# The w2 sums of the last ten tiles in 3.5 pairs of passes in place of four, with an order searched anew

## The chip, the cores and the metric

The kernel runs on one core of a Trainium2 chip. The metric is the device time of one execution in microseconds; the median of three runs of the kernel before is 189.86 us (189.66 to 190.07). Its work is bf16 with sums in f32, for one sequence of 2048 tokens and width 448.

## The reference, cut to what matters

```python
# part A: attention over the token itself and seven earlier ones at distance 2, 4, .. 14
q, k, v = split(layernorm(x) @ wqkv)                # 16 heads of 28
attn = softmax(mask(q . k[pos - 2*w] * 28**-0.5))   # w = 0..7
h = x + (attn . v[pos - 2*w]) @ wo
# part B, applied to y = layernorm(h); result: h + B(y)
g = gelu(layernorm(y) @ w1)                          # 448 channels
# channels 0-111 are read one token earlier, 112-223 one later, 224-335 two earlier, 336-447 two later
hs = concatenate([g0, g1, g2, g3]) @ w2              # 448 x 448
x1 = y + hs
out = h + x1 + gelu(layernorm(x1) @ w3) @ w4         # w3: 448 x 1792, w4: 1792 x 448
```

The change concerns `hs`: the product of the shifted channels with w2.

## The kernel before, in words

**Tiles and stages.** The 2048 tokens are 16 tiles of 128, or 4 token blocks of 512. Each block runs through N1 (layernorm), A1 (queries and keys), V (values), A2 (the products of queries and shifted keys on DVE, `qk_r`, summed on PE to logits), S (softmax), A3 (weights spread into a masked tile `bd_r`, multiplied with the gathered values `vw` on PE), O (wo and the residual), B1 (layernorm) and M (w1 and gelu). After that come five units of 2, 4, 4, 4 and 2 tiles (`UNITS`), each with B2 (w2, residual, layernorm statistics), T (normalisation and transposition), W3 (w3 and gelu) and B3 (w4, the final sum, the store). A name with a number (M2, T3) is a stage of that block or unit; a group such as M2's is four 112-channel pieces of a 512-token block.

**What is recorded and what sets the order.** The program doesn't issue instructions as it goes through its loops: it records operations, and `_Sched.arrange` puts them in the order of the list `ORDER`; the numbers in `OTHER` name operations that go to their second engine (a copy to DVE in place of ACT, say). Each engine runs its operations in that order and waits by semaphores: `sem_act` for ACT's work, `dsem_...` for a DMA. All loads, stores and transfers are issued by SP, in order. `arrange` adds two rules: a DMA transposition waits for the DMAs issued since the last one, and other DMAs with a fixed channel wait for the transpositions ahead of them. Buffers come from pools (eight PSUM banks; `NBD` buffers for `bd_r`). All instructions leave from one line, L991 in the profile, so that tiles tell groups apart.

**The names in profile rows.** `arena` is one large buffer that holds, among others, w3 (`w3_s`), w4, the queries and keys, and `gT`, the gelu's output of M: 112 partitions by four pieces by tokens, with two zero columns at each end. `w_s` is one of the small weights (w1 and w2 are both shown so). `actT` is a transposed activation, `lntm` a normalised one before transposition, `ps` a PSUM bank, `h3T` the gelu's output of W3.

**The sums of two tiles.** `duo` runs the sums of two tiles A and B in two halves. TensorE's rows are used as an upper half (partitions 0 to 63) and a lower one (64 and up), side by side: in the first half A's upper parts run beside B's lower parts, in the second B's upper beside A's lower. In B2 a tile has four upper parts of 64 rows and four lower parts of 48 rows (112 is 64 + 48), so two tiles take eight pairs of passes. The shift is a column offset in the read of `gT`:

```python
SHIFT = (-1, 1, -2, 2)
...
return [(gT[part, c, 2 + i * 128 + SHIFT[c]:130 + i * 128 + SHIFT[c]], (lambda lo, m, c=c: w2_s[part, c, lo:lo + m])) for c in range(4)]
```

**Loads.** The queue of first loads ends with w1, w2 and the first of two halves of w3 (`load_rows("w3", ...)`, 896 KB each); the second goes out at 49 us by its place in the order. `load_w4` loads w4 in two halves.

Of the kernel before, what the change touches and what calls it, by code (L numbers as in the profile page):

```python
# [8 lines left out]
BF16 = mybir.dt.bfloat16  # L9
# [3 lines left out]
TURN = {'A1': 'ttdd', 'B1': 'dddd', 'B2': 'tdddd'}  # L13
NORM = {'N0': 'vvvv', 'N1': 'avvv', 'B1': 'avvv', 'B2': 'avvvv'}
STATS = {'N1': 'vvva', 'B1': 'avaa', 'B2': 'avvvv'}
NQK, NBD, NLN, NACT, NSM, NO = 3, 4, 2, 4, 1, 6
POWER = {'N1': 'aaaa', 'B1': 'aaaa', 'B2': 'apapp'}
RESIDUAL = 'ttvv'
ORDER = """
# [29 lines left out]
"""  # L49
OTHER = """  # L50
88 184 456 482 483 486 539 540 546
"""
FULL = (4,)
FILL = (0, 0, 0, 0)
# [226 lines left out]
def bass_sequential_preLN__sliding_local_dilated__mixer_s_mlp__prompt_kernel(  # L281
    nc, A_x, A_wqkv, A_wo, B_x, B_w1, B_w2, B_w3, B_w4, out,
):
    _, SEQ, D = A_x.shape
# [6 lines left out]
    PADK = 16  # L291
# [5 lines left out]
    o2 = out.rearrange("b s d -> (b s) d")  # L297
    S = _Sched()
    KC = 112


    A_W3 = 0
# [8 lines left out]
    with ExitStack() as es:  # L311
        def sb(name, shape, dt):
            return es.enter_context(nc.sbuf_tensor(name, shape, dt))
# [10 lines left out]
        wo_s = sb("wo_s", [128, 4, D], BF16)  # L324
        w1_s = sb("w1_s", [128, 4, D], BF16)
        w2_s = sb("w2_s", [KC, 4, D], BF16)
        ident = sb("ident", [128, 128], BF16)
        zc = sb("zc", [128, 4, 2, 32], BF16)
        st6 = sb("st6", [128, 8, 6], F32)
# [31 lines left out]
        qT = arv(A_QG, 128, 4 * QGW).rearrange("p (c n) -> p c n", c=4)  # L361
        gT = arv(A_QG, KC, 4 * QGW).rearrange("p (c n) -> p c n", c=4)
        kk = [arv(A_KV + t * KVB, 128, 3 * KVW).rearrange("p (c n) -> p c n", c=3) for t in range(NST)]
        kr = [arv(A_KV + t * KVB + 3 * KVW, 128, 4 * KW).rearrange("p (j n) -> p j n", j=4) for t in range(NST)]
# [26 lines left out]
        def copy(out_ap, in_ap, either=True):  # L391

            if not either:
                return act(out_ap, in_ap, ACT.Copy)
            return S.add("act", "activation", out=out_ap, in_=in_ap, func=ACT.Copy, alts=[("dve", [("tensor_copy", dict(out=out_ap, in_=in_ap))])])
# [9 lines left out]
        def dma(chan, out_ap, in_ap, nbytes, eng="sp", **kw):  # L405
            return S.add(eng, "dma_start", chan=chan, nbytes=nbytes, out=out_ap, in_=in_ap, **kw)
# [45 lines left out]
        TOP, BOT = slice(0, 64), slice(64, 128)  # L452
# [212 lines left out]
        def phase_A1(t):  # L665
# [21 lines left out]
            X, Y = _Tile(P_bank), _Tile(P_bank)  # L687
            both = ((X, D - 64, ((0, 1, 2, 3), (0, 2, 3))), (Y, 2 * D - 64, ((0, 1, 3), (0, 1, 2, 3))))
            op = None
            for second in range(2):  # L690
# [9 lines left out]
                op = S.group("pe", [("matmul", kw) for _, kw, _ in specs], pe=[(n, "s", None) for _, _, n in specs])  # L700
# [3 lines left out]
                return Y(lambda v: v[64 * h:64 * h + 64, 0:256].rearrange("p (j n) -> p j n", j=4)[:, lo:lo + n, 64 - PADK:])  # L704

            copy(qT[:, 3, now:now + 256], X(lambda v: v[:, 0:256]))
            copy(kr[t][:, :, PADK:], Y(lambda v: v[:, 0:256].rearrange("p (j n) -> p j n", j=4)))
            copy(kr[t][64:128, :, 0:PADK], last(0, 0, 4), False)
            copy(kr[t][0:64, 1:4, 0:PADK], last(0, 1, 3), False)
            if t + 1 < NST:  # L710
# [148 lines left out]
        SHIFT = (-1, 1, -2, 2)  # L859
# [3 lines left out]
        def phase_B2(u):  # L863
            tiles = UNITS[u]
            summed = STATS["B2"][u] == "a"

            def group(i):
                b = _Tile(P_bank)

                def side(part):  # L870
                    return [(gT[part, c, 2 + i * 128 + SHIFT[c]:130 + i * 128 + SHIFT[c]], (lambda lo, m, c=c: w2_s[part, c, lo:lo + m])) for c in range(4)]

                def out():
                    kw = dict(accum_out=mv[:, 2, i, 0:1]) if summed else {}
                    dve("scalar_tensor_tensor", out=xb[i], in0=xin[:, i, :], scalar=rs_y[:, 1, 0, i:i + 1], in1=b(lambda v: v[:, 0:D]), op0=ALU.mult, op1=ALU.add, **kw)
                    if not summed:
                        ln_stats(2, xb[i], i)

                return (lambda lo, n: b(lambda v: v[:, lo:lo + n]), side(TOP), side(slice(64, KC))), out

            for i in tiles[::2]:
                (A, out_a), (B, out_b) = group(i), group(i + 1)
                duo(A, B, ((0, D),))
                out_a()
                out_b()
            ln = _Tile(P_ln)
            if summed:
                sums_stats(2, tiles, lambda i: xb[i], ln)
            S.tag = "T%d" % u
            norms = norms_of("B2", u, len(tiles))  # L890
            rstd(2, tiles[0], len(tiles), summed, norms, POWER["B2"][u])
            last = [normalize(2, i, ln, n, xb[i], TURN["B2"][u], summed, norms[n]) for n, i in enumerate(tiles)]
            for i in tiles:
                S.add("pool", "tensor_tensor", after=last, out=xb[i], in0=xb[i], in1=xin[:, i, :], op=ALU.add).block = True
            b2_a[u] = transposed(ln, TURN["B2"][u], len(tiles))
# [49 lines left out]

        def load_w4():

            w4_v = B_w4.rearrange("(f k) n -> k f n", k=128)
            for f in range(0, NF, 7):
                dma("w4%d" % f, w4_s[:, f:f + 7, :], w4_v[:, f:f + 7, :], 128 * 7 * D * 2)  # L950
# [82 lines left out]
```

## Time and profile before

| | before |
|---|---|
| median of 3 runs | 189.86 us (189.66 to 190.07) |
| profiled execution | 189.68 us |
| its span | 187.4 us |
| TensorE clock granted | 1.00 |
| PE, DVE, ACT, POOL busy | 179.5, 126.5, 119.2, 25.1 us |
| DMA | 17.70 MB, mean 94 GB/s |

The span runs from the first instruction to the last; the profiled execution's time holds 2.3 us more around it. "Busy" leaves out waits and the issue of DMAs; PE's busy time counts pairs of matmuls side by side once. A row of the timeline names start, duration, engine, operation, output, inputs, and behind x how many instructions; a row of DMAs the kilobytes of one and the median time from issue to landing.

### The profile page before, as it was taken

To read this page: it belongs to the slowest core of one execution; us is meant where nothing else is said; L and a number is where in the kernel's file an instruction comes from. 1 tells how busy PE (TensorE), PEld (TensorE's weight loads), DVE (VectorE), ACT (ScalarE), POOL (GpSimd) and SP (SyncE) were. 2 spreads that over 40 slices of the span, in tenths; PEclk is the share of its full clock that TensorE was granted. 3 is DMA by queue.
4 is the path that set the end of the run, shared out by engine and by line. 5 is a ranking of instruction groups with operands and counts; after the bars stand their busy time and mean duration, and the time that the engine had idled before them with its cause. 6 is when DMAs were issued, how large, how long until landed. Compare 5 with 4: busy or idle time off the path is not lost.

```text
span 187.4 us, 5753 instructions
## 1 busy us (share of the span) xinstructions
PE 179.5 (96%) x2506; PEld 100.1 (53%) x2506; DVE 126.5 (67%) x226; ACT 119.2 (64%) x286; POOL 25.1 (13%) x59
## 2 busy tenths in 40 slices
PE   4998998999899999999999999999999999999994
PEld 1574443444444555684444655565555555565873
DVE  6989999999999999988985153975980034000502
ACT  3559899899999999875498867062267022740250
POOL 4310000000000000435300000020029304300000
PEclk9999999999999999999999999999999999999999
DMA  5999435366355649603306000515007002400121
GB/s 152 331 301 231 143 66 103 86 140 122 84 187 106 123 94 269 192 2 60 57 3 136 3 3 0 112 27 115 3 0 161 3 0 68 114 0 3 40 84 49
DMA packets 32161, 17.70 MB, mean 94 GB/s; under 512 B 20888, under 2 KB 31624, under 8 KB 32136
## 3 DMA queue, kind: packets, MB, share of 16 engines
q1 hardware_dynamic: 32136, 17.34, 38.0%
q8 instruction: 19, 0.31, 0.7%
q14 instruction: 6, 0.05, 0.1%
HBM read 7.91 MB, written 1.84 MB: 52 GB/s over the span
## 4 chain that ended last, share of the span: by engine, by line
PE 85%; DVE 10%; ACT 3%; POOL 1%; issue 1%; POOLq 0%; DVEq 0%
PE ps L991 85%; DVE qk_r L991 5%; DVE bd_r L991 2%; ACT actT L991 1%; ACT arena L991 1%; DVE pb L991 1%; DVE mx L991 1%; POOL ls L991 1%; DVE ls L991 0%; ACT vt L991 0%; POOL ident L991 0%; DVE actT L991 0%; ACT mx L991 0%; DVE lntm L991 0%; DVE nm L991 0%
## 5 line engine op out<-in xcount | busy, mean ns | idle before, releaser
L991 PE MATMUL ps<-actT,arena 64*128 64x512 bf16 (+2 forms) x812 | 69.3, 326 | 1.3 <-ACT vt L991 0.6
L991 ACT ACTIVATE h3T<-ps 128x512 bf16<-128x512 f32 (+1 forms) x70 | 31.0, 515 | 35.8 <-PE ps L991 35.4
L991 PEld LDWEIGHTS ps<-actT,arena 64*128 64x128 bf16 (+1 forms) x812 | 37.8, 96 | 29.1 <-ACT arena L991 1.9
L991 PE MATMUL ps<-arena,h3T 64*128 64x448 bf16 (+2 forms) x434 | 44.8, 343 | 0.0
L991 DVE SCALAR_TENSOR_TENSOR qk_r<-ps,mrs,arena 128x448 bf16<-128x448 f32 (+1 forms) x17 | 10.7, 653 | 37.8 <-PE ps L991 37.7
L991 PEld LDWEIGHTS ps<-arena,h3T 64*128 64x128 bf16 (+1 forms) x434 | 25.0, 94 | 17.2 <-ACT h3T L991 0.2
L991 ACT ACTIVATE arena<-ps 128x512 bf16<-128x512 f32 (+6 forms) x65 | 29.9, 507 | 3.7 <-PE ps L991 3.1
L991 DVE TENSOR_TENSOR qk_r<-arena 128x4096 bf16<-128x4096 bf16 (+1 forms) x16 | 32.1, 2013 | 0.0
L991 POOL TENSOR_TENSOR arena<-arena,xin 128x448 f32<-128x448 f32 x16 | 16.2, 1033 | 55.1 <-DVE lntm L991 55.1
L991 DVE TENSOR_TENSOR bd_r<-arena,bmask 80x2048 bf16<-80x2048 bf16 x16 | 18.9, 1216 | 0.0
L991 PE MATMUL ps<-wo_s,actT 64*128 64x448 bf16 x128 | 14.2, 350 | 0.1
L991 ACT ACTIVATE actT<-ps 128x512 bf16<-128x512 f32 (+2 forms) x21 | 12.3, 639 | 2.9 <-PE ps L991 2.9
L991 PE MATMUL ps<-arena,actT 64*128 64x448 bf16 x112 | 12.9, 350 | 0.6 <-ACT actT L991 0.6
L991 PE MATMUL ps<-w_s,arena 64*128 64x448 bf16 (+1 forms) x128 | 13.3, 349 | 0.0
L991 PE MATMUL ps<-actT,w_s 64*112 64x512 bf16 x112 | 13.2, 377 | 0.0
L991 ACT ACTIVATE lntm<-xin,nm 128x448 bf16<-128x448 bf16 x16 | 10.6, 670 | 3.3 <-DVE nm L991 3.3
L991 ACT ACTIVATE rs_x<-mv,epsilon 128x4 f32<-128x4 f32 (+2 forms) x16 | 4.6, 294 | 12.0 <-DVE mv L991 11.9
L991 DVE SCALAR_TENSOR_TENSOR arena<-xin,rs_y,ps 128x448 f32<-128x448 bf16 x16 | 10.3, 669 | 1.5 <-PE ps L991 1.5
L991 DVE BATCH_NORM_STATS2 st<-xin 128x6 f32<-128x448 bf16 x16 | 9.2, 613 | 0.6 <-DMA xin<-in_A_x_dram 0.5
L991 PEld LDWEIGHTS ps<-actT,w_s 64*112 64x112 bf16 x112 | 7.2, 127 | 4.3 <-ACT arena L991 0.3
L991 PEld LDWEIGHTS ps<-w_s,arena 64*128 64x128 bf16 (+1 forms) x128 | 6.6, 94 | 5.4
L991 DVE TENSOR_SCALAR lntm<-arena,mv,rs_y 128x512 bf16<-128x512 f32 x14 | 6.9, 540 | 3.0 <-POOL rs_y L991 2.4
(71 smaller groups left out, 150.3 us busy)
## 6 DMA issues: line engine op xcount, KB each, us to landing
arena<-in_B_w_dram SPq DMA_DIRECT2D x2, 896.0 KB, 9.6
out_dram<-qk_r SPq DMA_DIRECT2D x15, 112.0 KB, 1.8
arena<-in_B_w_dram SPq DMA_DIRECT2D x2, 784.0 KB, 6.1
vw<-vt SPq DMA_DIRECT2D x4, 320.0 KB, 4.8
vw<-vt SPq DMA_DIRECT2D x4, 256.0 KB, 3.6
arena<-in_A_wqkv_dram SPq DMA_DIRECT2D x2, 448.0 KB, 4.6
xin<-in_A_x_dram SPq DMA_DIRECT2D x2, 448.0 KB, 6.8
xin<-in_A_x_dram SPq DMA_DIRECT2D x3, 224.0 KB, 5.3
```

Source lines behind the costliest of these rows:

```text
L991: inst = getattr(eng, meth)(**kw)
```

## The change

For units 2, 3 and 4 (ten tiles) the four lower parts of 48 rows are put together into three parts of 64: 4 x 48 = 192 = 3 x 64. Since TensorE's lower half takes its weights and data from partitions 64 to 127, seven transfers for each unit copy pieces of `gT`, shifted already, into a new buffer `ht`; and w2's rows are loaded a second time, in the same arrangement, as `w2_l`, by seven small loads in `load_w4`. Of two tiles A takes four upper parts and three packed ones, B three upper and four packed: the fourth packed part holds rows 0 to 63 of the fourth piece, in `ht` too. So two tiles take seven pairs of passes.

The other edits: `NBD` from 4 to 2 (which frees room for `ht` and `w2_l`); a copy of keys in A1 that could go to either engine stays on ACT; `ORDER` and `OTHER` are new. DVE has 3 operations fewer, ACT 3 more, SP 28 DMAs more (64 to 92), PE 10 instructions fewer (2506 to 2496).

```diff
-NQK, NBD, NLN, NACT, NSM, NO = 3, 4, 2, 4, 1, 6
+NQK, NBD, NLN, NACT, NSM, NO = 3, 2, 2, 4, 1, 6
...
-88 184 456 482 483 486 539 540 546
+182 438 482 483 546 552
...
+    LOWER = ((0, 64, 112, 0, 64), (1, 64, 80, 0, 112), (1, 80, 112, 1, 64), (2, 64, 96, 1, 96), (2, 96, 112, 2, 64), (3, 64, 112, 2, 80), (3, 0, 64, 3, 64))
...
+        w2_l = sb("w2_l", [128, 4, D], BF16)
+        ht = sb("ht", [128, 4, 512], BF16)
...
-            copy(kr[t][:, :, PADK:], Y(lambda v: v[:, 0:256].rearrange("p (j n) -> p j n", j=4)))
+            copy(kr[t][:, :, PADK:], Y(lambda v: v[:, 0:256].rearrange("p (j n) -> p j n", j=4)), False)
...
+            dense = u >= 2
+            n, first = 128 * len(tiles), 128 * tiles[0]
+            if dense:
+                for c, lo, hi, k, at in LOWER:
+                    dma("ht", ht[at:at + hi - lo, k, 0:n], gT[lo:hi, c, 2 + first + SHIFT[c]:2 + first + SHIFT[c] + n], (hi - lo) * n * 2)
+
+            def group(i, upper):
...
+                if dense:
+                    top = side(TOP, range(3 + upper))
+                    bot = [(ht[BOT, k, 128 * i - first:128 * i - first + 128], (lambda lo, m, k=k: w2_l[BOT, k, lo:lo + m])) for k in range(4 - upper)]
+                else:
+                    top, bot = side(TOP, range(4)), side(slice(64, KC), range(4))
...
-                (A, out_a), (B, out_b) = group(i), group(i + 1)
+                (A, out_a), (B, out_b) = group(i, True), group(i + 1, False)
...
+            for c, lo, hi, k, at in LOWER:
+                low = dma("w2l", w2_l[at:at + hi - lo, k, :], B_w2[KC * c + lo:KC * c + hi, :], (hi - lo) * D * 2)
+                low.odeps.add([op for op in S.ops if op.tag == "load" and op.is_dma][-1])
```

Three places show how it moves instructions. The first is PE where unit 2's w2 sums begin. Before, they follow the output projection of the last block (`wo_s`), wait for ACT alone, and go by eight matmuls a half (sixteen in a row where no wait stands between), with B3's (`h3T`) among them:

```order
L991 MATMUL ps<-wo_s,actT 128x448 x7
L991 MATMUL ps<-w_s,arena 128x448 [waits sem_act]
L991 MATMUL ps<-w_s,arena 128x448 x15
L991 MATMUL ps<-arena,h3T 128x448 [waits sem_dve]
L991 MATMUL ps<-arena,h3T 128x448 x13
```

Now, at the same place:

```order
L1009 MATMUL ps<-wo_s,actT 128x448 x7
L1009 MATMUL ps<-w_s,arena 128x448 [waits dsem_w2l,sem_act,dsem_ht]
L1009 MATMUL ps<-w_l,ht 128x448
L1009 MATMUL ps<-w_s,arena 128x448
L1009 MATMUL ps<-w_l,ht 128x448
L1009 MATMUL ps<-w_s,arena 128x448
L1009 MATMUL ps<-w_l,ht 128x448
L1009 MATMUL ps<-w_s,arena 128x448
L1009 MATMUL ps<-w_l,ht 128x448
L1009 MATMUL ps<-w_s,arena 128x448 [waits sem_act]
```

Upper passes (`w_s`, `arena`) and packed ones (`w_l`, `ht`) alternate, and the first waits for the transfers into `ht` and for `w2_l`. Between M2's last matmul and this place stand now 14 of W3's matmuls, 64 of the value sums and the 32 of `wo_s`.

The second is SP at w3's loads. Before, the load of the second half stands between two transpositions of B1 (the first half stands in the first queue, not shown):

```order
L991 DMA vw<-vt 80x4x512 [waits sem_act,dsem_turn1]
L991 DMA arena<-in_B_w_dram 128x2x1792
L991 DMA_TRANSPOSE actT<-lntm 128x16x128 [waits sem_dve,dsem_vwb0,dsem_w3b,sem_act]
L991 DMA_TRANSPOSE actT<-lntm 128x16x128 [waits dsem_turn3,sem_dve]
L991 DMA vw<-vt 16x3x512 [waits dsem_turn2]
L991 DMA vw<-vt 64x4x512
L991 DMA arena<-in_B_w_dram 128x7x448 [waits sem_pe]
```

Now:

```order
L1009 DMA_TRANSPOSE actT<-lntm 128x16x128 [waits sem_act,sem_dve,dsem_vwc0,dsem_vwa0,dsem_vwb0,dsem_vwp0]
L1009 DMA_TRANSPOSE actT<-lntm 128x16x128 [waits sem_dve,dsem_turn2]
L1009 DMA arena<-in_B_w_dram 128x2x1792 [waits dsem_turn3]
L1009 DMA arena<-in_B_w_dram 128x2x1792
L1009 DMA vw<-vt 16x512
L1009 DMA arena<-in_B_w_dram 128x7x448 [waits sem_pe]
L1009 DMA w_l<-in_B_w_dram 16x448
```

Both halves of w3 (128x2x1792) stand behind the second of those transpositions and wait for it to land; the first half of w4 (128x7x448) and the small loads of `w2_l` follow.

The third is SP where unit 2's transfers go out. Before there was nothing between a store and the next transposition:

```order
L991 DMA_TRANSPOSE actT<-lntm 128x16x128 [waits dsem_turn3,sem_dve]
L991 DMA out_dram<-qk_r 128x448
L991 DMA_TRANSPOSE actT<-lntm 128x16x128 [waits sem_dve]
L991 DMA_TRANSPOSE actT<-lntm 128x16x128 [waits dsem_turn0,sem_dve]
L991 DMA out_dram<-qk_r 128x448
```

Now seven transfers and a load of `w2_l` stand there:

```order
L1009 DMA out_dram<-qk_r 128x448 [waits sem_dve]
L1009 DMA ht<-arena 32x512 [waits sem_act]
L1009 DMA ht<-arena 64x512 [waits sem_act]
L1009 DMA w_l<-in_B_w_dram 32x448
L1009 DMA ht<-arena 16x512
L1009 DMA ht<-arena 48x512
L1009 DMA ht<-arena 16x512 [waits sem_act]
L1009 DMA ht<-arena 48x512 [waits sem_act]
L1009 DMA ht<-arena 32x512
L1009 DMA_TRANSPOSE actT<-lntm 128x16x128 [waits sem_dve]
L1009 DMA_TRANSPOSE actT<-lntm 128x16x128 [waits dsem_turn0,sem_dve]
```

The last three of them follow M2's last gelus. The two transpositions behind are that of the last token block's B1 and that of T2; unit 3's seven transfers stand behind the second, four of them behind a further wait for ACT.

More of the change, by code (lines that the diff above doesn't have):

```diff
@@ L865, in phase_B2, with side @@
             summed = STATS["B2"][u] == "a"
-            def group(i):
-                b = _Tile(P_bank)
-                def side(part):
-                    return [(gT[part, c, 2 + i * 128 + SHIFT[c]:130 + i * 128 + SHIFT[c]], (lambda lo, m, c=c: w2_s[part, c, lo:lo + m])) for c in range(4)]
+            dense = u >= 2
[4 more added lines that the diff above has]
+            def group(i, upper):
+                b = _Tile(P_bank)
+                def side(part, chunks):
+                    return [(gT[part, c, 2 + i * 128 + SHIFT[c]:130 + i * 128 + SHIFT[c]], (lambda lo, m, c=c: w2_s[part, c, lo:lo + m])) for c in chunks]
+                if dense:
[3 more added lines that the diff above has]
+                    top, bot = side(TOP, range(4)), side(slice(64, KC), range(4))
                 def out():
@@ L877, in out @@
                         ln_stats(2, xb[i], i)
-                return (lambda lo, n: b(lambda v: v[:, lo:lo + n]), side(TOP), side(slice(64, KC))), out
+                return (lambda lo, n: b(lambda v: v[:, lo:lo + n]), top, bot), out
             for i in tiles[::2]:
-                (A, out_a), (B, out_b) = group(i), group(i + 1)
+                (A, out_a), (B, out_b) = group(i, True), group(i + 1, False)
                 duo(A, B, ((0, D),))
```

59 rows, old and new, of the table ORDER are left out of this document.

## The prediction

> **What bounds the kernel now.** I read the page first: busy time by engine, the slices, the shares of the chain. The digits are tenths of a slice of 4.7 us.
>
> ```profile
> PE 179.5 (96%) x2506; PEld 100.1 (53%) x2506; DVE 126.5 (67%) x226; ACT 119.2 (64%) x286; POOL 25.1 (13%) x59
> PE   4998998999899999999999999999999999999994
> DVE  6989999999999999988985153975980034000502
> PEclk9999999999999999999999999999999999999999
> PE 85%; DVE 10%; ACT 3%; POOL 1%; issue 1%; POOLq 0%; DVEq 0%
> ```
>
> PE is busy for 96% of the span at full clock and carries 85% of the chain. DVE's slices are full up to about the twentieth and ragged behind it: the program has two halves with different limits. Where they part is told by the chain of waits in order of time (start, duration, engine, tile):
>
> ```profile
> 15.26 9.02 PE ps L991 x113
> ...
> 26.06 2.19 DVE qk_r L991
> ...
> 33.86 2.27 DVE bd_r L991 x2
> ...
> 48.30 28.23 PE ps L991 x502
> 76.55 0.61 ACT actT L991
> 77.15 0.14 issue
> 77.29 14.59 PE ps L991 x222
> 91.89 93.00 PE ps L991 x1082
> 184.92 0.45 DVE qk_r L991
> ```
>
> Up to 48 us the chain goes to and fro between PE and DVE (the products qk_r, the masked weights bd_r); from 48.30 it is PE, left once at 76.55 for an ACT copy. The windows cut there give busy time of PE, PEld, DVE, ACT, POOL, then clock, DMA share and GB/s:
>
> ```profile
> 0.00:24.30 24.30, 20.76 (x280) 11.22 (x282) 21.59 (x45) 16.21 (x43) 4.58 (x35) 1.00 0.82 224
> 24.30:48.30 24.00, 22.40 (x415) 10.33 (x412) 23.63 (x27) 22.43 (x63) 0.00 (x0) 1.00 0.48 101
> 48.30:77.30 29.00, 28.76 (x512) 14.63 (x513) 28.59 (x42) 28.11 (x67) 1.37 (x4) 1.00 0.66 166
> 77.30:91.90 14.60, 14.58 (x224) 9.90 (x224) 12.95 (x32) 8.56 (x20) 5.86 (x5) 1.00 0.24 48
> 91.90:184.90 93.00, 92.98 (x1082) 53.98 (x1082) 39.23 (x84) 43.83 (x96) 13.26 (x16) 1.00 0.19 45
> ```
>
> From 91.9 to 184.9 us PE is busy 92.98 of 93.00: PE waits for nothing, and the other engines are less than half busy. There, what is taken from PE shortens the kernel one for one. From 24.3 to 77.3 DVE is busy 52.22 of 53.00, PE 51.16 and ACT 50.54: three engines at their limit at once, so that order decides. PE's whole idle time before 91.9 is 3.54 + 1.60 + 0.24 + 0.02 = 5.40 us. The first of PE's waits is not to be had, since it stands ahead of its first matmul:
>
> ```profile
> PE ps L991 <- POOL ident L991: 2.6, 1, 2.6
> ```
>
> So a better order of the head can win at most 5.40 - 2.6 = 2.8 us.
>
> **The passes taken away.** The by-form groups (mean ns last but one) show that upper and lower passes of w2's sums take the same time whether they use 64 or 48 rows, and the timeline shows 48 in a row, with PE's next group behind:
>
> ```profile
> L991 PE MATMUL ps<-w_s,arena 48*128 48x448 bf16 x64 | 13.2, 349 | 0.0
> L991 PE MATMUL ps<-w_s,arena 64*128 64x448 bf16 x64 | 13.2, 349 | 0.0
> ```
>
> ```profile
> 127.03 4.71 PE L991 MATMUL ps<-w_s,arena 64*128 64x448 bf16 x48
> 131.57 0.39 PE L991 MATMUL ps<-actT,arena 64*128 64x512 bf16 x2
> ```
>
> From start to start 24 pairs take 131.57 - 127.03 = 4.54 us, 0.189 us a pair: upper and lower run side by side, and the pair is the unit of cost. Two tiles had 8 pairs and now have 7; ten tiles are five twos, so 5 pairs go: **5 x 0.189 = 0.95 us**. That matches the ten instructions by which PE's list is shorter (2506 to 2496). They stand in B2's units 2, 3 and 4, all behind 91.9 us. That the fuller lower passes cost more I hold at nothing: 48 and 64 rows are both 349 ns. A bound: were the passes not side by side, ten tiles would cost far more, but the new halves occupy the same two halves of the array as before.
>
> **The transfers added, at B2's units.** Unit 2 (tiles 6 to 9) reads columns of the third token block, so its transfers wait for the gelus of M2, the w1 sums of that block; unit 3's wait for M3's. The rows:
>
> ```profile
> 94.81 8.23 PE L991 MATMUL ps<-actT,arena 64*128 64x512 bf16 x74
> 102.97 1.40 PE L991 MATMUL ps<-bd_r,vw 80*32 80x64 bf16 x128
> 104.30 3.23 PE L991 MATMUL ps<-actT,w_s 64*112 64x512 bf16 x28
> 107.37 3.19 PE L991 MATMUL ps<-wo_s,actT 64*128 64x448 bf16 x32
> 110.39 1.68 PE L991 MATMUL ps<-w_s,arena 64*128 64x448 bf16 x16
> ```
>
> ```profile
> 106.92 2.06 ACT L991 ACTIVATE arena<-ps 112x512 bf16<-112x512 f32 x4 [0.79 <-PE ps L991]
> ```
>
> ```profile
> L991 SPq DMA_DIRECT2D vw<-vt x15: 577/634/1437, 30.0 to 73.4; - x15
> ```
>
> ```profile
> vw<-vt SPq DMA_DIRECT2D x4, 48.0 KB, 3.2
> ...
> vw<-vt SPq DMA_DIRECT2D x3, 16.0 KB, 3.1
> ```
>
> Nearest kin of an ht transfer (16 to 64 KB, chip memory to chip memory) is vw<-vt: 0.634 us of SP's queue for each issue, 3.1 to 3.2 us to landing. Behind the last matmul of the w1 sums that it needs, two gelus take 2 x 0.515 = 1.03 us, three transfers are issued (the last starts 1.27 us later), and it lands 3.1 us after: 5.4 us. The bound from below takes the fastest vw landing in the trace, 2.2 us: 4.5 us. As cover PE now has between those sums and the first packed pass 14 W3 matmuls, 64 of the value sums and 32 of the output projection: 14 x 8.16/74 + 64 x 1.33/128 + 3.02 = 1.54 + 0.67 + 3.02 = 5.2 us. The wait is between -0.7 (none) and +0.2 us. At unit 3 the cover is 56 W3 matmuls, 56 x 0.110 = 6.2 us, against 1.03 + four issues (1.90) + 2.2 to 3.1, 5.1 to 6.0 us: none, provided SP is free. It is held there by T2's transposition; four further issues stand between that and the four. Unit 4 has more cover, and its transfers wait for unit 3's last read of ht. I take **0** for all three and keep +0.4 (0.2 twice) by these rows, more if SP is late. Behind a waiting packed pass PE has everything that is left in its order, so such a wait is paid in full. Behind a waiting ht issue stand on SP the outputs and the next transposition; the outputs need not be soon.
>
> The Trainium skill, in "DMA: Bandwidth & Descriptors", section "Anatomy of one DMA", gives a transfer (measured there for those that GpSimd issues) a fixed cost of about 2.0 us and the rest by its bytes at 436 GB/s. By that estimate a 64 KB transfer lands in 2.15 us and unit 2 has 0.8 us to spare. The trace's 3.1 us for only 16 KB speaks against so short a time here; by either the sum stays.
>
> **w3 loaded late.** One of w3's two loads stood in the first load queue and the other went out at 49 us; now both stand behind the second token block's B1 transposition. Before, that transposition's issue ended, and SP was free again, shortly ahead of the first row here:
>
> ```profile
> 66.03 1.34 SPq L991 DMA_DIRECT2D vw<-vt  x2
> 67.41 0.61 SPq L991 DMA_DIRECT2D arena<-in_B_w_dram  x1
> ```
>
> ```profile
> 77.29 0.94 PE L991 MATMUL ps<-actT,arena 64*128 64x256 bf16 x14 [0.24 <-ACT actT L991]
> ```
>
> ```profile
> arena<-in_B_w_dram SPq DMA_DIRECT2D x1, 896.0 KB, 7.7
> ```
>
> The third row is the first matmul that needs w3; the last is the second half's own landing (in the stretch 49 to 57 us). Both halves issued from 66.0: if they run side by side and as fast as the best window of the trace (224 GB/s over 24.3 us), 1.835 MB take 8.2 us, some 1 to 2 us more for start and end: 75 to 76 us, in time. If the queue takes them one after the other, 7.7 us and then 5.5 (the row less 2.2 for start and end, the fastest vw landing): 79.2, which is **1.9 us late**. Nothing hides it but the work put ahead of W3's first matmul. I take 0, nearer the first: the row of 7.7 us was measured among gathers of vw. In return the first 24 us carry 0.9 MB less, and there the DMA share is 0.82; PE does wait in that stretch, 0.9 us beside the first wait. I take nothing for it.
>
> **The rest of the order.** DVE loses three operations to ACT (a copy of A10, one of V3, one of A33 and one of T0 go, one of A13 comes: net three), none on the chain after 91.9. bd_r has two buffers rather than four:
>
> ```profile
> L991 DVE TENSOR_TENSOR bd_r<-arena,bmask 80x2048 bf16<-80x2048 bf16 x16 | 18.9, 1216 | 0.0
> ```
>
> DVE fills one in 1.216 us and PE reads one in 1.40/4 = 0.35 us, so two are enough where PE comes at once; where it doesn't, DVE stands, and it has 0.78 us to spare in 53. Bounds of the head: -2.8 us (all of PE's idle time goes) to +2.4 us (DVE loses one product in two of the four blocks). I take **0**: no engine has much less to do there. The seven loads of w2's second copy, 0.6 us of SP each, lie ahead of T1's transposition:
>
> ```profile
> 86.55 1.87 SPq L991 DMA_TRANSPOSE actT<-lntm  x1
> ```
>
> SP's last vw issue starts at 73.4 (its row above) and this one at 86.55; in those 13 us 7 x 0.63 = 4.4 us more are hidden.
>
> **Sum.** 189.68 (the profiled execution, 187.4 of it span) - 0.95 = 188.73. The median of the runs is 189.86; I forecast **188.8**.
>
> **The rivals.**
> First, *the head gains too*. For: 2.8 us of idle time, fewer DVE operations, lighter early DMA. Against: DVE at 98% from 24 to 77 us. At half the ceiling the time is 187.4; range of the case 187.2 to 188.3.
> Second, *the transfers come late*: at units 2 and 3 PE waits at its first packed pass. For: covers of 5.2 and 6.2 us against up to 5.4 and 6.0. Against: the rows' lower ends. With 0.4 to 1.0 us of waits the saving is eaten: 189.2 to 189.8, no change.
> Third, the other side: *w3 lands late*. Place: PE's first W3 matmul; price: its landing less the time at which PE comes to it, 1.9 us in the serial case, giving 188.73 + 1.9 = 190.6. It decides from 0.95 us on: w3 landing after about 78.2 us makes the kernel slower. For: all of w3 in one stretch, with w4 behind it on the same queue; against: 8.2 us by the first window's rate. A head that loses DVE time to two bd_r buffers ends in the same range (up to 191).
> That the passes do not get fewer in time, though fewer in count, I give next to nothing: 349 ns twice.
>
> **Chances.** Forecast (188.3 to 189.4) 0.40; head gains 0.13; transfers late 0.16; w3 or the head's order late 0.31. A measurement of this kernel tells a change of about 0.2%, 0.38 us, from none. Faster: 0.40 + 0.13 = 0.53; same 0.16; slower 0.31. Range: the lower case down to 187.7 (part of it left out), the upper to 190.8, which takes in 190.6.
>
> **What would show it.** The group w_s,arena with the new w_l,ht must keep 0.189 us a pair, and the window that begins where PE stops waiting must be shorter by 0.95. A wait of PE's w_s,arena on a DMA into ht shows the second rival; a wait of ps<-actT,arena on in_B_w_dram near 77 us the third; PE idle before 77 us of over or under 5.4 us tells the head. I am wrong above all if PE's last wait-free stretch begins later than 91.9 by more than 0.5 us.

## The result, and the profile after

| | before | after |
|---|---|---|
| median of 8 runs each | 189.76 us | 191.37 us |
| ratio | 1 | 1.0087 (95% interval 1.0061 to 1.0114) |
| profiled execution, its span | 189.68, 187.4 us | 191.2, 189.5 us |

The changed kernel is slower by 1.6 us. Ratios here and below leave disturbed executions out, so a few of the medians lie a little above what their ratio says. The page of the changed kernel, engines, slices and chain:

```profile
PE 180.3 (95%) x2496; PEld 93.8 (49%) x2496; DVE 125.7 (66%) x223; ACT 120.4 (64%) x289; POOL 25.0 (13%) x59
PE   6899998997999999999997999999999999999994
DVE  6789899998999999989647437852086066000502
PEclk9999999999999999999999999999999999999999
PE 66%; DMA 12%; DVE 10%; ACT 8%; POOL 1%; issue 1%; SPq 1%
```

The engines' loads have hardly changed; the chain has. PE carries 66% of it and not 85%: transfers have 12%. PE's waits name them (sum, times, longest):

```profile
PE ps L1009 <- DMA actT<-lntm: 1.8, 2, 1.2
PE ps L1009 <- POOL ident L1009: 1.6, 1, 1.6
PE ps L1009 <- DMA vw<-vt: 1.0, 1, 1.0
PE ps L1009 <- DMA ht<-arena: 0.5, 1, 0.5
```

None of the three DMA rows was there before. (Of the first row's 1.8 us, 0.6 stands at 29.6 us, where before PE waited 0.6 us for ACT.) The windows say where. Ahead of 91.9 us PE is idle for 4.8 us in all, against 5.4 before; in the stretch behind it, where it was busy for 92.98 of 93.00 us, it is now busy for 91.22:

```profile
0.00:24.30 24.30, 21.77 (x284) 10.90 (x284) 20.39 (x43) 17.39 (x46) 4.57 (x35) 1.00 0.45 139
24.30:48.30 24.00, 21.90 (x432) 9.94 (x430) 23.09 (x28) 21.26 (x57) 0.00 (x0) 1.00 0.61 135
48.30:77.30 29.00, 29.00 (x466) 15.00 (x460) 28.64 (x40) 28.01 (x69) 0.79 (x2) 1.00 0.68 179
77.30:91.90 14.60, 14.42 (x266) 9.09 (x252) 13.44 (x32) 9.88 (x24) 6.60 (x8) 1.00 0.41 95
91.90:184.90 93.00, 91.22 (x1064) 47.32 (x1061) 39.03 (x81) 43.81 (x97) 13.05 (x15) 1.00 0.25 56
```

The timeline shows three places; the time in brackets is the idle time that the profile sees, and the row ahead tells when PE would have come without it:

```profile
44.68 0.35 PE L1009 MATMUL ps<-xin,ident 64*128 64x448 bf16 x2
46.02 0.42 PE L1009 MATMUL ps<-bd_r,vw 80*32 80x64 bf16 x32 [0.99 <-DMA vw<-vt]
...
99.22 2.32 PE L1009 MATMUL ps<-actT,arena 64*128 64x512 bf16 x20
102.74 2.58 PE L1009 MATMUL ps<-actT,w_s 64*112 64x512 bf16 x22 [1.20 <-DMA actT<-lntm]
...
109.45 3.21 PE L1009 MATMUL ps<-wo_s,actT 64*128 64x448 bf16 x32
113.12 0.36 PE L1009 MATMUL ps<-w_s,arena 64*128 64x448 bf16 x1 [0.46 <-DMA ht<-arena]
113.12 0.36 PE L1009 MATMUL ps<-w_l,ht 64*128 64x448 bf16 x1
113.32 0.35 PE L1009 MATMUL ps<-w_s,arena 64*128 64x448 bf16 x1
```

At 46 us PE comes 0.19 us after 44.68 (one pair) and begins at 46.02: 1.15 us lost. At M2 (the third block's w1 sums) the 20 W3 matmuls take 2.16 us from start to start, so PE comes at 101.38 and begins at 102.74: 1.36. At unit 2's first packed pass the output projection's 32 take 3.03, so PE comes at 112.48 and begins at 113.12: 0.64. Together 3.15 us; against that stand the 0.95 us of passes and 1.0 us of an earlier first matmul (the wait for `ident` is 1.6 and not 2.6). The net is 1.2 us of the 2.1 by which the spans differ (189.5 and 187.4); the profiled executions differ by 1.5 alone, because 1.7 us of the second lies outside its span and 2.3 of the first. The other 0.9 us has no such place. Adding up, tile by tile, the times from the start of one matmul to that of the next, without the idle time, shows it spread over the other groups: `ps<-actT,arena`, say, takes 66.6 us and not 66.0. Why is not shown. The packed passes themselves cost what was forecast: `w_s` and `w_l` begin together, 0.19 to 0.20 us a pair, and by the same addition w2's sums take 11.4 us and not 12.3, 0.9 less.

Why does M2 wait? Its input is the transposition of the third block's B1. The DMA view from its issue to M2, and then its last two microseconds alone (from 100.55 us):

```profile
DMA  0000000039999999999999997130000000000000
q1 hardware_dynamic: 2080, 0.52, 45.0%
q8 instruction: 1, 0.02, 1.0%
issues: line engine op xcount, KB each, median us to landing
...
actT<-lntm SPq DMA_TRANSPOSE x1, 5.9
```

```profile
DMA packets 6, 0.02 MB, mean 8 GB/s; under 512 B 5, under 2 KB 5, under 8 KB 5
...
q8 instruction: 1, 0.02, 2.8%
q1 hardware_dynamic: 5, 0.00, 0.3%
```

The slices of the first view are 0.15 us: the transposition's data are through by 100.7, but it lands at 102.6, 5.9 us after its issue; the 17 others of full size in the two traces take 4.3 to 4.5, one of them 4.9. In the last 2 us only one packet of instructions of 16 KB begins, and five small ones of the queue that holds the transposition. The packets of q8 are PE's by their number (19 in the kernel before, for 5,012 matmuls and weight loads, some 260 each). The trace also holds the 16 signals by which this transposition tells of its completion: 15 come between 4.25 and 4.40 us after its issue, the last at 5.94. That is **theory A**: a load of PE's instructions, asked for while a transposition runs, can go ahead of its completion and delay it by 1.6 us. It need not: of the same kernel's other transpositions, one landed after 4.36 and one after 4.33 us although such a packet began 3.7 and 3.9 us after the issue, as here (3.9). **Theory B**: the loads of `w1` and `w2`, now between gathers of `vw`, make PE wait at 46. The rival to both: the order itself is slower, or the transfers of the packing are.

The Trainium skill has a rule that fits the first: in "DMA: Bandwidth & Descriptors", section "Queues, rings and completion order", the increment of a semaphore lands only after every earlier write of that DMA engine, across its queues. The 5.9 us and the single late signal agree with it.

### The profile page after: what moved, and what is told of

The parts are those of the page before. It is cut to its first block, busy times and chain, and to the rows that moved or that the text cites. A ratio compares the mean times of both kernels' runs of the same rounds, so it can differ in the third digit from the quotient of the medians.

```text
span 189.5 us, 5776 instructions
## 1 busy us (share of the span) xinstructions
PE 180.3 (95%) x2496; PEld 93.8 (49%) x2496; DVE 125.7 (66%) x223; ACT 120.4 (64%) x289; POOL 25.0 (13%) x59
## 4 chain that ended last, share of the span: by engine, by line
PE 66%; DMA 12%; DVE 10%; ACT 8%; POOL 1%; issue 1%; SPq 1%
PE ps L1009 66%; DMA actT<-lntm 5%; DMA vw<-vt 4%; ACT arena L1009 4%; DVE lntm L1009 3%; ACT actT L1009 2%; DVE st L1009 2%; DMA xin<-in_A_x_dram 2%; ACT lntm L1009 1%; POOL rs_y L1009 1%; DMA ht<-arena 1%; DVE arena L1009 1%; DVE qk_r L1009 1%; DVE xin L1009 1%; SPq L1009 1%
## 5 line engine op out<-in xcount | busy, mean ns | idle before, releaser
L1009 PE MATMUL ps<-actT,arena 64*128 64x512 bf16 (+2 forms) x812 | 70.4, 326 | 1.3 <-DMA actT<-lntm 0.6
L1009 ACT ACTIVATE h3T<-ps 128x512 bf16<-128x512 f32 (+1 forms) x70 | 30.5, 524 | 35.5 <-PE ps L1009 35.3
L1009 PEld LDWEIGHTS ps<-actT,arena 64*128 64x128 bf16 (+1 forms) x812 | 34.8, 96 | 33.0 <-PE ps L1009 1.7
L1009 PEld LDWEIGHTS ps<-arena,h3T 64*128 64x128 bf16 (+1 forms) x434 | 22.8, 94 | 19.2 <-ACT h3T L1009 0.2
L1009 ACT ACTIVATE actT<-ps 128x512 bf16<-128x512 f32 (+2 forms) x23 | 13.9, 636 | 2.1 <-PE ps L1009 1.9
L1009 PE MATMUL ps<-actT,w_s 64*112 64x512 bf16 x112 | 13.9, 379 | 1.3 <-DMA actT<-lntm 1.2
L1009 PE MATMUL ps<-w_s,arena 64*128 64x448 bf16 x83 | 12.4, 349 | 0.5 <-DMA ht<-arena 0.5
L1009 PEld LDWEIGHTS ps<-w_s,arena 64*128 64x128 bf16 x83 | 5.7, 95 | 6.3 <-DMA ht<-arena 1.2
```

The lines of the kernel that those rows point to most:

```text
L1009: inst = getattr(eng, meth)(**kw)
```

## The experiments

### First four: each suspect alone

e1 cuts the warm-up matmuls, which adds 154 instructions to PE's stream and no work, and so moves every later instruction load:

```diff
-            return mm(busy(), ident[:], bass.AP(ident, 0, [[128, 128], [0, 4], [1, 128]]), True, True, 512, after)
+            return mms([(busy(lambda v: v[:, 0:64]), ident[:], ident[:, 0:64], True, True, 64, None) for _ in range(8)], after)
```

> The changed kernel with each of TensorE's 11 warm-up matmuls of 512 columns cut into 8 of 64: about the same work before the first data, 154 instructions more in TensorE's stream, so that each later 16 KB load of its instructions falls some microseconds earlier (the one at 100.6 us to about 94.5). Theory A (that instruction load holds back the last packets of the B1 transposition of the third block, which lands 5.9 us after its issue in place of 4.3): the transposition takes 4.3 to 4.4 us, PE's wait at M2 of 1.2 us goes, and the time falls by 1.2 to 1.9 us, to 189.5 to 190.2. Rival (the wait belongs to the order: the transposition is issued too late for where M2 now stands): wait and time stay, 191.1 to 191.7.

e2 moves the loads of wo, w1 and w2 in ORDER:

```diff
-50 55 56 20 51 6 52
+50 55 56 20 21 22 23 24 25 26 51 6 52
```

> The changed kernel with the loads of wo, w1 and w2 back behind the first load of wo, as in the kernel before, and not among the gathers of vw at 29 to 37 us. Theory B (these loads stand ahead of two gathers of vw on SP's queue, which land 8.3 us after their issue, and PE waits 1.0 us for one at 46): that wait goes, and the time falls by 0.6 to 1.6 us, to 189.8 to 190.8. Rival (DVE sets the pace up to 77 us anyway, so that PE only waits elsewhere): less than 0.3 us, 191.1 to 191.6.

e3 undoes the packing (ORDER and OTHER are renumbered without the 28 transfers):

```diff
-            dense = u >= 2
+            dense = False
...
-            for c, lo, hi, k, at in LOWER:
+            for c, lo, hi, k, at in ():
```

> The changed kernel's order with the packing undone: four pairs of passes in the last ten tiles too, no transfers into ht, no second load of w2. Theory (packing itself gives 0.95 us of PE and costs a wait of 0.5 to 0.6 us at unit 2; the loss is in the rest of the order): 0.3 to 0.5 us slower than the changed kernel, 191.6 to 192.0. Rival (the transfers are what makes the changed kernel slow): 189.5 to 190.5.

e4 is e1 and e2 together.

> The changed kernel with both edits, short warm-up matmuls and the early loads of wo, w1 and w2. If theories A and B both hold and add: 1.8 to 3.2 us less than the changed kernel, 188.2 to 189.6, at or below the kernel before. If only one holds, as that one alone.

| | median us | ratio to before (interval) | M2's transposition | M2's wait |
|---|---|---|---|---|
| after | 191.37 | 1.0087 (1.0061 to 1.0114) | 5.9 us | yes |
| e1 | 190.91 | 1.0084 (1.0054 to 1.0114) | 4.3 | none |
| e2 | 191.59 | 1.0112 (1.0078 to 1.0145) | 5.9 | yes |
| e3 | 192.48 | 1.0123 (1.0073 to 1.0173) | 5.9 | yes |
| e4 | 190.9 | 1.0072 (1.0045 to 1.0099) | 4.3 | none |

As theory A has it, M2's wait comes and goes with the instruction load. But the time didn't follow. e1's DMA view from 87 to 97 us and its timeline show why:

```profile
q8 instruction: 1, 0.02, 0.5%
q14 instruction: 1, 0.01, 0.4%
issues: line engine op xcount, KB each, median us to landing
vw<-vt SPq DMA_DIRECT2D x1, 320.0 KB, 3.3
actT<-lntm SPq DMA_TRANSPOSE x2, 5.2
```

```profile
93.33 2.98 PE L1009 MATMUL ps<-actT,arena 64*128 64x512 bf16 x26 [1.32 <-DMA actT<-lntm]
```

The load moved from 100.6 to 91.2 us, onto T1's transposition, which now takes 6.0 (the mean of the two in this stretch is 5.2), and PE waits 1.3 us for that. In e2 the wait for `vw` is gone from PE's list, and a load falls on T2's transposition (6.0 us), where PE loses 1.1; its time is what its rival said. e3 is too uncertain to read.

### Where can the loads go? e5 to e8

e5 cuts six warm-up matmuls in halves (12 instructions more), e7 all of them into six (110 more), by the edit of e1; e8 is e2 with e5's; e6 is e1's edit in the kernel before.

```diff
-                keep_busy()
+                keep_busy(parts=2 if n < 6 else 1)
```

> The changed kernel with six of the warm-up matmuls cut in halves: the same columns, 12 instructions more in TensorE's stream, each later 16 KB load of instructions a little earlier. Theory A, made narrower (an instruction load that is asked for between a transposition's issue and its last data waits for the data, goes ahead of its completion and makes it land 1.6 us later; by the counts of the changed kernel's trace a shift of 6 to 14 instructions takes the loads off the transpositions of T1, B1 of the third and fourth block and T2): all these land 4.3 to 4.4 us after their issue, PE waits for none of them over 0.4 us, and the time is 189.4 to 190.3 us. Rival (what remains is the order's own, the loads of instructions only move the wait about): 190.7 to 191.4.

> The kernel before with the short warm-up matmuls of e1 (154 instructions more). By the counts of its trace this puts instruction loads on the transpositions of T1, of the third block's B1 and of T2. Theory A with margins (the kernel before reaches these transpositions' readers 1.4 to 2.5 us after they land, the changed one 0.2 to 0.9 us after): they land up to 1.6 us later, and the time rises by no more than 0.5 us. Rival (a slow transposition costs its 1.6 us in any order): 1.5 us or more.

> The changed kernel with the warm-up matmuls cut into six of 64 columns: 110 instructions more. By the same counts only the transpositions of the fourth block's A1 and of the first block's B1 are hit. Theory A: these two land up to 1.6 us late, the later ones in 4.3 to 4.4, and the time is 189.6 to 190.6 us, between e5 and e1. Rival: as e1, 190.9, or more.

> The changed kernel with the early loads of wo, w1 and w2 (e2) and the shift of e5. Theories A and B together (in e2 the wait for vw at 46 us went, but two later transpositions were slow at 5.9 us): no wait for vw, no slow transposition on PE's way, 188.6 to 189.6 us. If A holds and B doesn't: as e5. If neither: 191 or more.

e5: 192.4 us, 1.0117 (1.0074 to 1.0161); e6: 191.41, 1.0082 (1.0051 to 1.0113); e7: 192.49, 1.0163 (1.011 to 1.0215); e8: 190.4, 1.0051 (1.0026 to 1.0076). By the time, theory A was missed in all four. In e5 and e8 twelve instructions were not enough: M2's transposition still took 5.9 and 5.8 us. In e5 a load (at 111.5 us) also met the last of unit 2's transfers: 15 of its 16 signals had come by 112.1 us, the last came at 113.7, and PE waited 2.0 us for `ht`. In e7 M2's transposition took 4.3 us, while those of the fourth block's A1 and the first block's B1, which the expectation had named, took 5.9 and 6.1 (the granted clock of this profile was 0.991, so only landings are read from it). e6 did not test the part on margins: the transpositions that it was to delay, of T1, the third block's B1 and T2, took 4.7, 4.3 and 4.3 us. Still the kernel before, with the same computation and 154 instructions more, loses 0.8%. Its profile has 0.7 us more of waits ahead of 9 us, and its timeline shows what may be another way in which a load costs time:

```profile
103.15 1.28 PE L991 MATMUL ps<-bd_r,vw 80*32 80x64 bf16 x127
105.42 0.19 PE L991 MATMUL ps<-bd_r,vw 80*32 80x64 bf16 x1 [0.98 <-issue]
```

PE stops for 1 us inside a row of 128 equal matmuls that wait for nothing, one short of its end: most likely it has run out of instructions. The instructions of these short matmuls go at some 190 a microsecond (127 with their weight loads in 1.33 us), so that a packet's 260 last 1.4 us; the packet at 103.0 us began 2.4 us before PE went on. In the three other traces with such a stop (e1, e4, e17) PE goes on 2.2 to 2.6 us after a packet began. No run here takes the cause away to prove it.

### Making room in the order: e9 to e11

e9 puts M2 behind 2.8 us of other PE work, and 28 matmuls of B3 ahead of the packed passes; e10 is that with e2's edit, e11 is e10 without packing. The PE part of the edit:

```diff
-625 416 412 417 485 488 626 413 637 494 491 638 496 500 497 501 668 676 669 677 653 654
+625 485 488 626 637 638 416 412 417 413 494 491 496 500 497 501 653 654 668 676 669 677
```

> The changed kernel with one stretch of the order redone by hand: the third block's w1 sums (M2) stand behind 64 of the last value sums and 20 of W3's matmuls that stood behind or among them (2.8 us of PE), the first 28 matmuls of B3's unit 1 stand ahead of unit 2's w2 sums, and two gathers of vw go out ahead of T1's transposition. Theory A with margins (M2 now comes 0.3 us after a transposition of ordinary length has landed, so that any 1.6 us of an instruction load is paid; unit 2's packed passes come as their transfers land): no wait at M2 and under 0.3 us at unit 2 whatever the transposition takes, 189.2 to 190.2 us. Rival (the next transposition, the fourth block's, sets the pace, and the wait only moves to M3 or to W3's unit 2): 190.8 to 191.4.

> e9 with the early loads of wo, w1 and w2 of e2. Theories A and B (the wait for vw at 46 us goes as well): 188.3 to 189.4 us, 0.4 to 1.1 us under e9. If DVE sets the pace up to 77 us: as e9.

> e10 with the packing undone (four pairs of passes, no transfers into ht, no second load of w2). Theory (the packing by itself is worth the 0.95 us of its five pairs where its transfers are covered): 0.6 to 1.2 us slower than e10. Rival (behind it PE waits for the transposition of T2 instead, or the transfers cost what the passes save): within 0.3 us of e10.

All three are slower still: 194.39 us, 1.0249 (1.0208 to 1.029); 194.02, 1.0227 (1.0201 to 1.0253); 194.2, 1.0235 (1.0203 to 1.0266). The waits at M2 and at the packed passes did go, and the rival's took their place: in e10 PE waits 1.7 us at M3 for the fourth block's transposition and 1.1 for T2's; 0.7 us for `bd_r` at 101.6 and 1.0 for ACT at 110.0 are new as well. The edit itself made the fourth block's transposition late (issued at 121.6 against 119.8), so these runs show how little slack the next wait has, and not what M2's is worth. e11 lies within 0.2 us of e10, as its rival said: the packing gains nothing in this order.

### Moving the load without the neighbours: e12 to e14

e12 leaves the order alone. It cuts 44 matmuls between 64 and 85 us in two, so that only loads behind them move:

```diff
-                duo(A, B, ((0, 512),))
+                duo(A, B, ((0, 512),), cuts=2 if t == 1 else 1)
...
-                duo(A, B, ((0, D),))
+                duo(A, B, ((0, D),), cuts=2 if t == 2 and il == 0 else 1)
```

> The changed kernel with 44 matmuls between 64 and 85 us cut in two by columns (the second block's w1 sums, and half of the third block's output projection): the same columns, 88 instructions more, so that the head keeps its instruction loads where they are and those behind 85 us come earlier, the one at 100.6 us to about 95, between the two transpositions of T1 and of the third block. Theory A: both land 4.3 to 4.4 us after their issue, M2's wait goes, 189.6 to 190.4 us. Rival (loads of instructions only move the wait about, as in e1 and e5): 190.7 to 191.6.

e13 adds e2's edit, and e14 is e13 without packing.

> e12 with the early loads of wo, w1 and w2 of e2. Theories A and B together: 188.6 to 189.7 us. If B is hidden by DVE: as e12.

> e13 with the packing undone (four pairs of passes, no transfers into ht, no second load of w2). Theory (where nothing else is late, packing is worth its 0.95 us less the wait for ht of up to 0.6): 0.3 to 1.0 us slower than e13. Rival (the transposition of T2 sets when W3's unit 2 begins, and the packing saves nothing): within 0.3 us of e13.

| | median us | ratio to before (interval) |
|---|---|---|
| e12 | 190.55 | 1.0033 (1.0007 to 1.0059) |
| e13 | 189.97 | 1.0023 (0.9995 to 1.0051) |
| e14 | 189.33 | 0.9983 (0.9964 to 1.0001) |

e12's DMA view from 96.5 to 102.7 us has no instruction packet any more, and M2 begins right behind the 20 W3 matmuls:

```profile
q1 hardware_dynamic: 2171, 0.60, 49.9%
issues: line engine op xcount, KB each, median us to landing
...
actT<-lntm SPq DMA_TRANSPOSE x1, 4.3
```

```profile
99.08 2.32 PE L1011 MATMUL ps<-actT,arena 64*128 64x512 bf16 x20
101.24 2.54 PE L1011 MATMUL ps<-actT,w_s 64*112 64x512 bf16 x22
```

With 88 instructions more and the same order, more than half of the loss is gone (1.0087 at first, 1.012 when measured again in e17, to 1.0033). So theory A is shown for M2's wait. What that wait alone is worth is not separated: e12's wait for `vw` is shorter too (0.35 us), and the one for `ht` longer (1.0 us). e12 and e13 end 0.15 and 0.3 us above the ranges of theory A. B is not settled as a gain: e13's PE reaches W3 0.7 us earlier than e12's (76.9 against 77.6), but the ratios overlap.

e14 was the surprise: without packing the kernel is not slower by up to 1.0 us but faster by 0.6. The timelines of e13 and e14 at unit 2's w2 sums:

```profile
107.21 3.19 PE L1011 MATMUL ps<-wo_s,actT 64*128 64x448 bf16 x32
111.23 0.36 PE L1011 MATMUL ps<-w_s,arena 64*128 64x448 bf16 x1 [0.83 <-DMA ht<-arena]
```

```profile
106.82 3.19 PE L1010 MATMUL ps<-wo_s,actT 64*128 64x448 bf16 x32
109.85 2.44 PE L1010 MATMUL ps<-w_s,arena 64*128 64x448 bf16 x24
```

e14's sums follow the projection after 3.03 us, e13's after 4.02: the wait for `ht` costs 1.0 us, as much as all five pairs save. The saving itself is there: e13 begins these sums 1.4 us behind e14 and ends its span 0.5 behind. The 0.4 us by which e14 is ahead already at the projection arose before 20 us, where PE's rows are the same; why, and so whether packing in this order loses anything beyond what it saves, is not shown.

### Why the transfers are late: e15 to e17

SP's timeline in e13 shows the eight issues of unit 2, without a gap. That they, and not the landing, make the last transfer late is **theory C**:

```profile
103.75 1.79 SPq L1011 DMA_DIRECT2D ht<-arena  x2
105.59 0.59 SPq L1011 DMA_DIRECT2D w_l<-in_B_w_dram  x1
106.22 3.65 SPq L1011 DMA_DIRECT2D ht<-arena  x5
```

e15 is e13 with the load of `w_l` (530) moved out of this row, to its six others; e16 also puts 14 matmuls of B3 ahead of the packed passes; e17 is the changed kernel again.

```diff
-664 667 530 665 666
+664 667 665 666
```

> e13 with one load moved: the 28 KB of w2's second copy that stood among unit 2's seven transfers goes out with its six others. In e13 SP issues these eight without a pause from 103.8 to 109.9 us and PE waits 0.8 us for the last one. Theory C (SP's time for issues, 0.6 us each, not the landing, makes unit 2's transfers late): the wait shrinks by about 0.6 us, the time by 0.4 to 0.7 us against e13, ratio to the kernel before 0.998 to 1.001. Rival (the transfers wait for the gelus or for the landing): within 0.2 us of e13.

> e15 with 14 matmuls of B3's unit 1 (1.3 us of PE) ahead of unit 2's first packed pass. Theory C: no wait for ht at all, 0.7 to 1.1 us less than e13, ratio to the kernel before 0.994 to 0.998, under e14's 0.998. Rival (unit 2's sums now end later, so does the transposition of T2, and PE waits for it at W3's unit 2): as e15 or slower.

> The changed kernel itself, beside the others on one chip: ratio to the kernel before 1.006 to 1.011, as measured first.

e15: 189.67 us, 1.0001 (0.9978 to 1.0024); e16: 189.39, 0.9997 (0.9978 to 1.0016); e17: 191.96, 1.012 (1.0081 to 1.0159), all on one chip. e15's wait shrinks, to 0.6 us in PE's list and 0.7 from start to start. That is 0.3 us less and not 0.6, as is SP's row: the seven issues still take 5.8 us and not 6.1, since one of them took 1.5. In e16 the wait is gone, and as the rival said others came in its place:

```profile
PE ps L1011 <- POOL ident L1011: 1.6, 1, 1.6
PE ps L1011 <- DMA actT<-lntm: 1.1, 2, 0.6
PE ps L1011 <- DVE lntm L1011: 1.0, 1, 1.0
```

```profile
122.88 2.85 PE L1011 MATMUL ps<-actT,w_s 64*112 64x512 bf16 x22 [0.51 <-DMA actT<-lntm]
127.98 1.88 PE L1011 MATMUL ps<-actT,arena 64*128 64x512 bf16 x15 [0.28 <-DVE qk_r L1011]
```

Of the 1.1 us of the second row, 0.6 is at 29.7 us, as in the changed kernel. New are the 0.5 at M3, for the fourth block's transposition, and 0.3 at W3's unit 2, where T2's transposition lands 0.1 us before PE goes on; from start to start 0.7 and 0.4, together more than the 0.7 that was won at unit 2. The 1.0 us are at the start, at 6.7 us, where no edit reaches. So the wait for `ht` does follow SP's row of issues, as theory C has it, and in this trace what e16 wins there is waited for at the next transpositions. No version here is clearly faster than the kernel before; e14, which does without packing, comes nearest.

## Why the prediction was wrong, point by point

- *What bounds the kernel.* PE at full clock, with no wait in its list behind 91.9 us: that was read rightly. What failed is the step drawn from it, "what is taken from PE shortens the kernel one for one". That PE didn't wait there in one order said nothing of how close it came to waiting. Before, M2 began 2.1 us after its transposition had landed (issue 97.8, landing 4.4 us later, M2 at 104.3):

```profile
actT<-lntm SPq DMA_TRANSPOSE x1, 4.4
```

  In the new order PE would come at 101.4, 0.4 us after an ordinary landing. No term of the sum asked when each transposition lands against the place to which its reader was moved.
- *The passes taken away, 0.95 us.* The size was right: w2's sums take 0.9 us less. e13 against e14 shows the price: 1.0 us of wait at unit 2.
- *The transfers added, at nothing, at most 0.2 us at unit 2.* The mechanism was named, the size was not: 0.64 us in the changed kernel, 1.0 in e13. The step reckoned with three issues behind the last gelu and 3.1 us of landing. The landing was shorter (in e13 from 109.3 to 111.2, 1.9 us; here the 2.0 us of the Trainium skill's "DMA: Bandwidth & Descriptors", "Anatomy of one DMA", were nearer than the row of `vw`), but SP had eight issues of 0.6 us in a row, two of them doubled, and was not free when the gelu ended. At unit 3 the forecast of no wait held.
- *w3 loaded late, the rival for a slower kernel.* It did not happen. The two loads, issued at 67.0 and 67.4 us, landed at 73.1 and 75.4, 2.4 us ahead of W3's first matmul (77.8). The row has the median of the two:

```profile
arena<-in_B_w_dram SPq DMA_DIRECT2D x2, 896.0 KB, 7.1
```

- *The rest of the order, 0 in the head.* Up to 96 us that was fair: 1.0 us won at the start, in the wait for `ident` that the prediction held not to be had, and 1.15 lost at 46. The largest single loss, 1.36 us at M2, was in no rival. Its cause, an instruction load on a transposition, is shown by M2's wait going in e1, e4, e7 and e12 to e16 and staying in e2, e3, e5, e8 and e17, which keep M2's place and the load. (In e8 and e17 the profile puts the wait down to DVE's `bd_r`, which ended within 0.1 us of the landing.) That such a load would delay it there could not be read from the trace of before, where all nine transpositions of full size land after 4.3 to 4.5 us.
- *The range* ended at 190.8 because the slower cases were priced as one late load each; three small waits together came to 3.15 us.

Open: where the 0.9 us of the span beyond the three waits comes from, how much of the `vw` wait at 46 us is lost for good, and what decides whether an instruction load delays the transposition that it meets.

## What to carry to other kernels

An engine that is busy for 96% and waits for nothing may still be close to a wait: before moving its work, list for each transfer that it needs when it lands and when the engine will come in the new order, and keep room for a late landing. Work that is fed by DMAs pays for the issue time of every one of them on its queue, in a row, and 0.6 us times the number is the first thing to reckon. A result of 1% in a kernel of thousands of instructions can hang on where the loads of the instructions themselves fall, so an order that was found good must be measured again after any edit that changes their number.

## What the runs showed of the hardware that was not expected

- PE's instructions come as DMA packets of 16 KB (q8). Of the 171 transpositions of full size in all 19 traces, 19 took 5.6 to 6.1 us where most take 4.3, and in each of them such a packet began 2.9 to 4.1 us after the issue. In 14 of the 19, 15 of the 16 signals came in time and the last some 1.5 us later. But a packet that began 3.7 to 4.3 us after the issue left 17 others at 4.3 to 4.9 us.
- In rows of short matmuls PE can stop without a wait that the profile shows, most likely for want of instructions: 0.98 us in e6, 1.09 us in e17 at 45 us, in the profile as a wait for "issue" inside a group of equal matmuls.
- An issue of a DMA on SP takes 0.6 us, and now and then twice that or more (the first two of unit 2 in e13 take 0.58 and 1.17 us, one of e15 1.5).
- The kernel before, with nothing but its warm-up matmuls cut smaller, was slower by 0.8% (e6).
